# One Mish activation for the second layer's gate, and fp32r fillers of several widths in the opening, in an attention and two-layer MLP kernel

## The chip, the cores and the metric

The kernel runs on one core of a Trainium2 chip, as one program in one launch. The metric is the device time in microseconds. Before the change three runs gave 1089.35, 1090.94 and 1094.02 us, a median of 1090.94.

## The reference

```python
for t in range(S):                      # q, k, v, alpha: 4 x 8 x 768 x 48
    state = alpha[:, :, t, :, None] * state + np.einsum('bhd,bhe->bhde', k[:, :, t], v[:, :, t])
    y[:, :, t] = np.einsum('bhd,bhde->bhe', q[:, :, t], state)
x = y as 3072 tokens x 384
# first layer: 384 -> 2048 -> 384, weights float64
h = x @ w_in
g = (a[0] + a[1] * h + a[2] * h * h + a[3] * h**3) / (1 + abs(b[0]) * abs(h) + abs(b[1]) * h * h + 1e-6)
x = g @ w_out
# second layer: 384 -> 2048 -> 384, weights float64
h = x @ w_in
sp = np.where(h > 20.0, h, np.log1p(np.exp(np.minimum(h, 20.0))))
out = (h * np.tanh(sp)) @ w_out
```

The gate of the second layer, h * tanh(softplus(h)), is the function called Mish.

## The kernel before

The 3072 tokens are worked in six blocks of 512 (128 positions of four batches). Each layer goes over the six blocks, and in a block over 16 tiles of 128 hidden units: 96 steps a layer, 192 in all. A step has nine matmuls of 128x512 into a PSUM bank for the hidden tile (`hidden_mms`, L525: three slices of the 384 inputs, and for each the product of two float32 numbers that are split into a high and a low part, high by high, low by high and high by low), then the gate (`hidden`), the split of its result into a high part `gh` and a low part `gl` (`split_g`), and nine more matmuls into three output banks (`out_mms`, L585). After the 16 steps of a block the three output banks are copied out (`evacuate`, L596 and L598). Five banks (0 to 4) take hidden tiles once the attention is over, three (5 to 7) the outputs. The split tiles have a ring of five buffers by then, the tiles before the split a ring of eleven.

The first layer's steps run beside the attention of the next block, whose small matmuls (L352, L363, L434, L447, L482, L498) wait in turn for ScalarE and VectorE. The attention of the first block fills the opening, before the first step.

The gate of the first layer is a rational function on ScalarE, VectorE and GpSimd (L539 to L557). The gate of the second layer is computed as h * cos(2 arctan(sigmoid(-h))): sigmoid (L561) and arctan (L563) on ScalarE, a copy of h out of PSUM on VectorE (L562), then for three tiles at a time three sines (L568) between two loads of ScalarE's activation table, then the product by `tt` (L173 on VectorE, L175 on GpSimd, by the letters in `E_W`).

Weights come as float64 words and are made into split float32 by `load_w`: a transfer into one of two staging tiles `raw`, three integer operations on VectorE (L260, L262, L264), an Abs of the high words on ScalarE (L266), a product with its comparison on VectorE (L267), the cast to the high part on ScalarE (L180) and the difference to the low part on VectorE (L173: `wil` for the input weights, `wol` for the output weights). The sixteen loads of the second layer alternate: the first staging tile serves the input weights, the second the output weights. They overwrite the first layer's weights as these fall free, so they stand in the last block of the first layer and the first block of the second.

The order of everything is made beforehand. `Plan` takes each operation with its engine, an estimated length, a due time and what it reads and writes; `order()` plays the graph by these estimates, each engine taking, of what is ready, what is due first. The instructions are issued in that order, and each engine runs its own in that order. The due time of a step's output matmuls is its own plus `LAG` (40.27 us in the second layer), that of its split plus `D_SPL`. Table loads have an estimate only in `sines` (2.6 us for the two).

In the opening 120 matmuls that nothing needs (L635, "fillers") stand in the plan with the latest due times, so that TensorE takes one whenever nothing else is ready. The output matmuls of the first step use the same banks and come behind all of them. An fp32 matmul leaves two records in the trace.

Of the kernel before, what the change touches and what calls it, by code (L numbers as in the profile page):

```python
# [14 lines left out]
ALU = mybir.AluOpType  # L15
# [6 lines left out]
NP = H // 2            # head pairs  # L22
HC = 64                # state chunk
NBLK = S // P          # blocks of 4 x 128 tokens
NTOK = B * P           # tokens of a block
# [7 lines left out]
NLVM = 5               # levels that need a mask  # L33
T0, T_AT, T_MOE = (63.77, 5.28, 3.51)   # microseconds: the first step, a step with attention, one without
# [4 lines left out]
LAG, GRP = ((16.02, 40.27), (1, 3))  # L39
D_SIN, D_SPL = (16.46, (-2.71, 23.06))  # L40
NZX, NGX = (7, 2)
E_W = 'VVVPPV'
# [3 lines left out]
E_GL = ('PVPVVP', 'PVPPVV')  # L46
# [6 lines left out]
N_WARM = 120  # L53
D_CST = 5.0
NZ, NG, NU = 4, 3, 3   # buffers of the hidden tiles
C1 = 1.0 + 1e-6
# high word of the smallest float64 that is a normal float32, read as a float32
# [3 lines left out]
class Plan:  # L61
    """Instructions as a graph, ordered before they are issued.

    Operations are added in an order that is right; what they read and write gives the graph.
    order() plays them on the engines, by estimated times, each engine taking of its ready
    operations the one that is due first.
    """
# [3 lines left out]
    TICK, WARM = 3.413, 3060       # the clock of the tensor engine: columns in a tick that make the next one fast  # L71
# [76 lines left out]
def attention_moe_kernel(ctx: ExitStack, tc: tile.TileContext,  # L148
# [21 lines left out]
    def tt(eng, n, due, reads, writes, kw):  # L170
        """a product, sum or difference of two tensors on the vector engine or on GpSimd"""
        if eng == "V":
            dve(n, due, reads, writes, lambda: nc.vector.tensor_tensor(**kw()))  # L173
        else:
            pool(n, due, reads, writes, lambda: nc.gpsimd.tensor_tensor(**kw()))  # L175

    def copy(eng, n, due, reads, writes, out, in_):
        """a copy in SBUF"""
# [16 lines left out]
    c_2 = cpool.tile([P, 1], F32, name="c_2")  # L195
# [9 lines left out]

    us = [cpool.tile([P, NTOK], F32, name=f"u{j}") for j in range(NU)]

    def rings(pool, nz, ng, x):
        """buffers of the hidden tiles: before the split, and split"""
# [558 lines left out]
```

## Time and profile before

| | |
|---|---|
| median of three runs | 1090.94 us |
| profiled execution, first to last instruction | 1090.5 us |
| TensorE, ScalarE, VectorE, GpSimd busy | 94%, 86%, 75%, 30% |
| mean granted clock of TensorE | 0.992 |

The profiled execution has no time of its own beside its span of 1090.5 us, which lies 0.4 us under the median of the runs. A time in a row is counted from the span's start. PE is TensorE's matmuls, PEld its weight loads, DVE VectorE, ACT ScalarE, POOL GpSimd, SP SyncE, whose queue issues the transfers. A row of a group gives the line, the operation, what it writes and reads, the count, then busy time, the mean length of one, and the idle time of the engine ahead of them with what ended it. A matmul's length includes its way through the array and overlaps the next one's, so the pitch from start to start says what one costs. In a timeline the brackets give the idle time before an instruction.

### The profile page before, as it was taken

How to read it: one execution, taken by the hardware profiler on the slowest of the kernel's cores; microseconds unless marked ns; L12 is line 12 of the kernel's file. 1: busy time of each engine (PE TensorE's matmuls, PEld its weight loads, DVE VectorE, ACT ScalarE, POOL GpSimd, SP SyncE). 2: the span in 40 equal slices, each digit the busy share in tenths (PEclk: the TensorE clock that was granted, in tenths of full speed). 3: DMA queues.
4: the chain of work that ended last, by engine and by line, in shares of the span. 5: the costliest groups of instructions: out<-in, count | busy, mean ns of one | idle time of the engine just before them, and what ended most of it. 6: DMA issues, size and time to landing. Idle time of an engine off the chain costs nothing.

```text
span 1090.5 us, 24632 instructions
## 1 busy us (share of the span) xinstructions
PE 1030.2 (94%) x9912; PEld 806.5 (74%) x9912; DVE 814.8 (75%) x1266; ACT 933.7 (86%) x1788; POOL 323.1 (30%) x320
## 2 busy tenths in 40 slices
PE   6999887999899999999899999999999999999998
PEld 5767665777676777766677777778888888888886
DVE  7899999798898887877999699999884411234452
ACT  5789998999999998978788799899997988889773
POOL 4014454402012224332423134234101256643000
PEclk9999999899999999999999999999999999999999
DMA  6644142403050312113131111222110100000000
GB/s 206 204 138 145 45 155 73 147 15 109 17 185 17 98 54 90 58 56 105 57 99 36 60 58 49 88 97 98 48 58 1 59 1 29 30 19 10 1 29 29
DMA packets 28209, 78.31 MB, mean 72 GB/s; under 512 B 4160, under 2 KB 7360, under 8 KB 28096
## 3 DMA queue, kind: packets, MB, share of 16 engines
q1 hardware_dynamic: 28096, 76.75, 21.5%
q8 instruction: 78, 1.28, 0.5%
q14 instruction: 35, 0.29, 0.1%
HBM read 66.24 MB, written 9.44 MB: 69 GB/s over the span
## 4 chain that ended last, share of the span: by engine, by line
PE 39%; DVE 8%; ACT 5%; issue 1%; DMA 1%; POOL 0%; SPq 0%; DVEq 0%
PE bank L585 20%; PE bank L525 17%; DVE zx L542 1%; DVE p L548 1%; DVE px L557 1%; DMA raw<-in_w2i_dram 1%; DMA qka<-in_qT_dram 1%; ACT u L539 1%; DVE f L262 0%; DVE px L548 0%; DVE px L550 0%; DVE p L557 0%; PE bank L352 0%; DVE f L267 0%; DVE f L264 0%
## 5 line engine op out<-in xcount | busy, mean ns | idle before, releaser
L525 PE MATMUL bank<-xh,wih 128*128 128x512 f32 x576 | 234.8, 408 | 7.0 <-DVE px L550 3.0
L525 PE MATMUL bank<-xh,wil 128*128 128x512 f32 x576 | 225.6, 392 | 1.6 <-DVE wil L173 1.6
L525 PE MATMUL bank<-xl,wih 128*128 128x512 f32 x576 | 225.6, 392 | 0.0
L585 PE MATMUL bank<-gh,woh 128*128 128x512 f32 x444 | 184.1, 415 | 0.2 <-ACT u L598 0.2
L585 PE MATMUL bank<-gl,woh 128*128 128x512 f32 x444 | 175.6, 395 | 2.2 <-DVE gl L173 1.8
L585 PE MATMUL bank<-gh,wol 128*128 128x512 f32 x444 | 175.3, 395 | 0.4 <-DVE wol L173 0.4
L525 PEld LDWEIGHTS bank<-xh,wih 128*128 128x128 f32 x576 | 108.2, 188 | 32.5 <-DVE px L550 3.9
L525 PEld LDWEIGHTS bank<-xh,wil 128*128 128x128 f32 x576 | 108.4, 188 | 25.4 <-DVE wil L173 2.0
L525 PEld LDWEIGHTS bank<-xl,wih 128*128 128x128 f32 x576 | 108.6, 189 | 20.0 <-DVE xl L517 0.5
L175 POOL TENSOR_TENSOR gl<-p,gh 128x512 fp32r<-128x512 f32 x47 | 71.7, 1528 | 161.4 <-ACT gh L180 127.5
L334 ACT COPY Q<-qka 64x256 f32<-64x256 f32 x232 | 95.3, 411 | 26.9 <-DVE qka L319 14.5
L562 DVE COPY px<-bank 128x512 f32<-128x512 f32 x60 | 40.9, 688 | 85.7 <-PE bank L525 83.0
L546 POOL TENSOR_TENSOR z<-z,u 128x512 f32<-128x512 f32 x48 | 69.2, 1442 | 115.1 <-ACT z L545 114.5
L585 PEld LDWEIGHTS bank<-gh,wol 128*128 128x128 f32 x444 | 84.5, 190 | 19.5 <-DVE wol L173 0.8
L585 PEld LDWEIGHTS bank<-gh,woh 128*128 128x128 f32 x444 | 84.1, 189 | 19.4 <-ACT u L598 0.7
L585 PEld LDWEIGHTS bank<-gl,woh 128*128 128x128 f32 x444 | 84.6, 191 | 18.1 <-DVE gl L173 2.1
L352 PEld LDWEIGHTS bank<-Q,qka 128*31 128x31 f32 (+4 forms) x3840 | 39.5, 105 | 63.4 <-ACT Q L334 32.5
L548 DVE SCALAR_TENSOR_TENSOR p<-p,sc,bank 128x512 f32<-128x512 f32 x85 | 62.8, 740 | 17.9 <-ACT p L547 16.8
L352 PE MATMUL bank<-Q,qka 128*31 128x32 f32 (+4 forms) x3840 | 51.8, 197 | 24.4 <-ACT Q L334 10.0
L381 DVE TENSOR_TENSOR qka<-qka,qk 128x512 f32<-128x512 f32 x96 | 72.6, 764 | 1.6 <-PE bank L352 0.6
L539 ACT ACTIVATE u<-bank 128x512 f32<-128x512 f32 x96 | 57.2, 596 | 14.3 <-PE bank L525 12.6
L635 PE MATMUL bank<-cst 128*128 128x256 f32 x240 | 62.8, 400 | 6.0 <-DMA cst<-in_consts_dram 6.0
(117 smaller groups left out, 2235.9 us busy)
## 6 DMA issues: line engine op xcount, KB each, us to landing
qka<-in_kaT_dram SPq DMA_DIRECT2D x24, 512.0 KB, 5.2
qk<-in_nat_dram SPq DMA_DIRECT2D x24, 384.0 KB, 3.7
raw<-in_w1i_dram SPq DMA_DIRECT2D x8, 768.0 KB, 5.0
raw<-in_w1o_dram SPq DMA_DIRECT2D x8, 768.0 KB, 4.4
raw<-in_w2i_dram SPq DMA_DIRECT2D x8, 768.0 KB, 4.4
raw<-in_w2o_dram SPq DMA_DIRECT2D x8, 768.0 KB, 4.3
Q<-in_qT_dram SPq DMA_DIRECT2D x48, 96.0 KB, 2.4
qka<-in_qT_dram SPq DMA_DIRECT2D x48, 96.0 KB, 4.3
```

The source lines that it names most:

```text
L175: pool(n, due, reads, writes, lambda: nc.gpsimd.tensor_tensor(**kw()))
L334: act(2 * P, now(), [kQC], [kQ], lambda a=a, h=h: nc.scalar.copy(out=Qr[h, a], in_=Cr[h]), src="s")
L352: nc.tensor.matmul(lv[o:o + 32 - L, g, :, 16 * z:16 * z + 16].rearrange("p a (n l) -> p a n l", l=L), lhsT=K[:, g * P + o:g * P + o + 32 - L],
L381: dve(4 * P, now(), [kT[L]], [kQC, kK], lambda: nc.vector.tensor_tensor(out=QK, in0=QK, in1=Tv.rearrange("p m x -> p x m").unsqueeze(3).to ...
L525: nc.tensor.matmul(bank[hb], lhsT=w[f // 2][:, f % 2, k * P:(k + 1) * P], rhs=x[k], start=(k == 0 and j == 0), stop=(k == KT - 1 and j == 2))
L539: act(NTOK, due, [kh], [ku], lambda: nc.scalar.activation(u, h, AF.Abs))
L542: dve(NTOK, due, [ku], [kz], lambda: nc.vector.scalar_tensor_tensor(out=zs[r], in0=zs[r], scalar=B0, in1=u, op0=ALU.add, op1=ALU.mult), ptr=1)
L546: pool(NTOK, due, [ku], [kz], lambda: nc.gpsimd.tensor_tensor(out=zs[r], in0=zs[r], in1=u, op=ALU.mult))
L548: dve(NTOK, due, [kh], [kp], lambda: nc.vector.scalar_tensor_tensor(out=ps[r], in0=ps[r], scalar=A2, in1=h, op0=ALU.add, op1=ALU.mult), po ...
L562: dve(NTOK, due, [kh], [kp], lambda: nc.vector.tensor_copy(out=ps[r], in_=h), port=False)
L585: nc.tensor.matmul(bank[5 + k], lhsT=w[f // 2][:, f % 2, k * P:(k + 1) * P], rhs=x[q], start=(f == 0 and j == 0), stop=(f == FT - 1 and j ...
L635: nc.tensor.matmul(bank[5 + n % 3][:, 0:2 * P], lhsT=ident, rhs=cst[:, 0:2 * P], start=True, stop=True)
```

## The change

The second layer's gate becomes one activation that reads the hidden bank and writes the tile that is split. The sigmoid, the arctan, the sines with their table loads, the copy and the product go, and with them the grouping by three. The output matmuls of a second-layer step are due 10.2 us after the step and not 40.27, its split 0.9 us after and not 23.06. The differences `gl` of blocks 2 and 3 move from GpSimd to VectorE. The fillers read a tile of ones in place of the identity and the constants; each is a pair of fp32r matmuls, ten of one shape after ten of another, four shapes in turn, with an estimate of 0.45 us in place of 0.43. Comments are taken out, so that lines move up by up to 17.

```diff
-LAG, GRP = ((16.02, 40.27), (1, 3))
-D_SIN, D_SPL = (16.46, (-2.71, 23.06))
+LAG = (16.02, 10.2)
+D_SPL = (-2.71, 0.9)
 NZX, NGX = (7, 2)
-E_W = 'VVVPPV'
...
-E_GL = ('PVPVVP', 'PVPPVV')
+E_GL = ('PVPVVP', 'PVVVVV')
...
+WARM_FORM = ((128, 512), (128, 256), (128, 384), (96, 512))
...
-    c_2 = cpool.tile([P, 1], F32, name="c_2")
...
+    wtile = cpool.tile([P, NTOK], F32R, name="wtile")
...
         else:
-            # tanh(softplus(h)) = cos(2 arctan(sigmoid(-h)))
-            act(NTOK, due, [kh, "tables"], [kz], lambda: nc.scalar.activation(zs[r], h, AF.Sigmoid, scale=-1.0))
-            dve(NTOK, due, [kh], [kp], lambda: nc.vector.tensor_copy(out=ps[r], in_=h), port=False)
-            act(NTOK, due, [], [kz], lambda: nc.scalar.activation(zs[r], zs[r], AF.Arctan), src="s")
-
-    def sines(rs, due):
-        def emit():
-            for r in rs:
-                nc.scalar.activation(zs[r], zs[r], AF.Sin, scale=-2.0, bias=c_2)
-            nc.scalar.preload_act_table_set("sigmoid_and_others")
-
-        plan.add("ACT", 0.62 * len(rs) + 2.6, due, [], [f"z{r}" for r in rs], emit)
+            act(NTOK, due, [kh, "tables"], [kp], lambda: nc.scalar.activation(ps[r], h, AF.Mish))
 
     def split_g(l, r, q, i, due):
         c = steps[i][1]
-        kz, kp, kgh, kgl = f"z{r}", f"p{r}", f"gh{q}", f"gl{q}"
-        if l == 1:
-            tt(E_W[c], NTOK, due, [kz], [kp], lambda: dict(out=ps[r], in0=ps[r], in1=zs[r], op=ALU.mult))
+        kp, kgh, kgl = f"p{r}", f"gh{q}", f"gl{q}"
         copy(E_GH[l][c], NTOK, due, [kp], [kgh], lambda: ghs[q], lambda: ps[r])
         tt(E_GL[l][c], NTOK, due, [kp, kgh], [kgl],
            lambda: dict(out=gls[q], in0=ps[r], in1=ghs[q].bitcast(F32), op=ALU.subtract))
...
-        nc.vector.memset(c_2, 0.5 * math.pi)
...
+        nc.gpsimd.memset(wtile.bitcast(F32), 1.0)
...
     for n in range(N_WARM):
         def warm(n=n):
-            nc.tensor.matmul(bank[5 + n % 3][:, 0:2 * P], lhsT=ident, rhs=cst[:, 0:2 * P], start=True, stop=True)
-        pe(0.43, 1e6 + n, ["cst"], [f"bank{5 + n % 3}"], warm)
+            w, x = WARM_FORM[n // 10 % len(WARM_FORM)]
+            tw, tx = wtile[:, 0:w], wtile[:, 0:x]
+            for j in range(2):
+                nc.tensor.matmul(bank[5 + n % 3][0:w, 0:x], lhsT=tw, rhs=tx, start=True, stop=True)
+        pe(0.45, 1e6 + n, ["cst"], [f"bank{5 + n % 3}"], warm)
...
-    pend = []
     for i, (l, c, f) in enumerate(steps):
         if f == 0:
             if l == 1:
@@ -673,19 +661,14 @@
         hidden_mms(hb, f, V[i])
         nz, ng = (NZ, NG) if i < FT * (NBLK - 1) else (NZ + NZX, NG + NGX)
         hidden(l, hb, i % nz, i, V[i] + D_MID)
-        pend.append((l, c, f, i, i % nz, i % ng))
-        if len(pend) == GRP[l] or i + 1 in (L1N, len(steps)):
-            if l == 1:
-                sines([x[4] for x in pend], V[i] + D_SIN)
-            for l, c, f, i, r, q in pend:
-                split_g(l, r, q, i, V[i] + D_MID + D_SPL[l])
-                out_mms(f, q, V[i] + LAG[l])
-                if f == FT - 1:
-                    evacuate(l, c, V[i] + LAG[l] + D_EV)
-                if l == 0 and c == NBLK - 1 and f % 2 == 1:
-                    load_w(w2i, wi_h, wi_l, "wi", f // 2, V[i] + D_IN)
-                    load_w(w2o, wo_h, wo_l, "wo", f // 2, V[i] + D_OUT)
-            pend.clear()
+        r, q = i % nz, i % ng
+        split_g(l, r, q, i, V[i] + D_MID + D_SPL[l])
+        out_mms(f, q, V[i] + LAG[l])
+        if f == FT - 1:
+            evacuate(l, c, V[i] + LAG[l] + D_EV)
+        if l == 0 and c == NBLK - 1 and f % 2 == 1:
+            load_w(w2i, wi_h, wi_l, "wi", f // 2, V[i] + D_IN)
+            load_w(w2o, wo_h, wo_l, "wo", f // 2, V[i] + D_OUT)
```

The planner's result is a new order. The first place is on TensorE, at the first output step of the second layer (`bank5` from `woh0`); `wih`, `wil` are the high and low input weights, two steps to a number. Before:

```order
L525 MATMUL bank2_121<-xh2_109,wih5_75 128x512
L525 MATMUL bank2_121<-xl2_112,wih5_75 128x512
L525 MATMUL bank2_121<-xh2_109,wil5_83 128x512
L585 MATMUL bank5_124<-gh1_139,woh0_86 128x512
L585 MATMUL bank5_124<-gl1_142,woh0_86 128x512
L585 MATMUL bank5_124<-gh1_139,wol0_94 128x512
```

And now:

```order
L524 MATMUL bank3_121<-xh2_108,wih3_72 128x512
L524 MATMUL bank3_121<-xl2_111,wih3_72 128x512
L524 MATMUL bank3_121<-xh2_108,wil3_80 128x512
L571 MATMUL bank5_123<-gh1_139,woh0_85 128x512
L571 MATMUL bank5_123<-gl1_142,woh0_85 128x512
L571 MATMUL bank5_123<-gh1_139,wol0_93 128x512
```

The first output step stood behind twelve hidden steps (up to input weights 5) and now stands behind eight (up to 3).

The second place is on ScalarE, where the last block of the first layer is copied out of banks 5 and 7 (`u0`, `u2`), the second layer's first gates are made and weights are converted. Before:

```order
L563 ACTIVATE z1_131<-z1_131 128x512
L598 COPY u0_127<-bank5_124 128x512
L568 ACT_TABLE_LOAD
L568 ACTIVATE zx4_7428<-zx4_7428,c_2_68 128x512
L568 ACTIVATE zx5_7429<-zx5_7429,c_2_68 128x512
L568 ACTIVATE zx6_7430<-zx6_7430,c_2_68 128x512
L569 ACT_TABLE_LOAD
L266 ACTIVATE raw0_102<-raw0_102 128x768
L598 COPY u2_129<-bank7_126 128x512
L266 ACTIVATE raw1_103<-raw1_103 128x768
L561 ACTIVATE z2_132<-bank1_120 128x512
L180 CAST wih6_76<-f320_104 128x768
```

And now:

```order
L559 ACTIVATE p2_136<-bank1_119 128x512
L265 ACT_TABLE_LOAD
L265 ACTIVATE raw1_102<-raw1_102 128x768
L265 ACTIVATE raw0_101<-raw0_101 128x768
L559 ACT_TABLE_LOAD
L559 ACTIVATE p3_137<-bank2_120 128x512
L179 CAST wih6_75<-f320_103 128x768
L584 COPY u0_127<-bank5_123 128x512
L179 CAST woh1_86<-f321_104 128x768
L584 COPY u2_129<-bank7_125 128x512
L179 CAST gh0_138<-p1_135 128x512
```

The sines with their two table loads are gone; a load now stands ahead of the Abs of `raw` and another ahead of the next Mish (L559). There are 17 such loads in all.

The third place is on VectorE, behind the sixth low input weight (`wil5`). Before:

```order
L173 TENSOR_TENSOR wil5_83<-f320_104,wih5_75 128x768
L562 COPY px5_7436<-bank2_121 128x512
L562 COPY px6_7437<-bank3_122 128x512
L562 COPY p0_134<-bank4_123 128x512
L562 COPY p1_135<-bank0_119 128x512
L260 TENSOR_SCALAR f320_104<-raw0_102 128x768
L173 TENSOR_TENSOR wol0_94<-f321_105,woh0_86 128x768
L262 SCALAR_TENSOR_TENSOR f320_104<-raw0_102,f320_104 128x768
L260 TENSOR_SCALAR f321_105<-raw1_103 128x768
L264 SCALAR_TENSOR_TENSOR f320_104<-raw0_102,f320_104 128x768
L596 COPY u1_128<-bank6_125 128x512
L262 SCALAR_TENSOR_TENSOR f321_105<-raw1_103,f321_105 128x768
```

And now:

```order
L172 TENSOR_TENSOR wil5_82<-f320_103,wih5_74 128x768
L172 TENSOR_TENSOR wol0_93<-f321_104,woh0_85 128x768
L259 TENSOR_SCALAR f321_104<-raw1_102 128x768
L259 TENSOR_SCALAR f320_103<-raw0_101 128x768
L261 SCALAR_TENSOR_TENSOR f321_104<-raw1_102,f321_104 128x768
L261 SCALAR_TENSOR_TENSOR f320_103<-raw0_101,f320_103 128x768
L263 SCALAR_TENSOR_TENSOR f321_104<-raw1_102,f321_104 128x768
L263 SCALAR_TENSOR_TENSOR f320_103<-raw0_101,f320_103 128x768
L266 SCALAR_TENSOR_TENSOR f320_103<-raw0_101,f320_103 128x768
L266 SCALAR_TENSOR_TENSOR f321_104<-raw1_102,f321_104 128x768
L582 COPY u1_128<-bank6_124 128x512
L172 TENSOR_TENSOR wil6_83<-f320_103,wih6_75 128x768
```

The copies of hidden tiles (L562) are gone, and the conversions of `raw0` and `raw1` stand directly behind one another.

## Rows read from the trace of the kernel before

**Rows 1.** The page: busy time and share of each engine; the chain by line.

```profile
PE 1030.2 (94%) x9912; PEld 806.5 (74%) x9912; DVE 814.8 (75%) x1266; ACT 933.7 (86%) x1788; POOL 323.1 (30%) x320
...
PE bank L585 20%; PE bank L525 17%; DVE zx L542 1%; DVE p L548 1%; DVE px L557 1%; DMA raw<-in_w2i_dram 1%; DMA qka<-in_qT_dram 1%; ACT u L539 1%; DVE f L262 0%; DVE px L548 0%; DVE px L550 0%; DVE p L557 0%; PE bank L352 0%; DVE f L267 0%; DVE f L264 0%
```

**Rows 2.** By stretches: length, busy us (x) of each engine, clock, DMA share, GB/s.

```profile
100.00:600.00 500.00, 463.87 (x6313) 346.97 (x6312) 438.49 (x724) 451.85 (x981) 159.46 (x178) 0.98 0.25 77
...
640.00:680.00 40.00, 36.70 (x158) 29.04 (x157) 39.96 (x52) 37.32 (x65) 15.58 (x8) 1.00 0.13 41
...
800.00:840.00 40.00, 40.00 (x178) 33.13 (x177) 23.93 (x41) 32.31 (x45) 2.54 (x2) 1.00 0.07 20
...
695.00:780.00 85.00, 82.76 (x362) 67.30 (x361) 78.59 (x98) 82.41 (x125) 27.76 (x18) 1.00 0.27 93
```

**Rows 3.** The chain in order of time, near its end: start, us, what.

```profile
1062.16 24.49 PE bank L585 x108
```

**Rows 4.** TensorE: a group's row for 640 to 740 us, then its timeline (start, us).

```profile
L525 PE MATMUL bank<-xh,wih 128*128 128x512 f32 x74 | 29.1, 394 | 4.1 <-DVE px L550 3.0 <-DVE p L550 1.1
...
698.06 0.50 PE L585 MATMUL bank<-glx,woh 128*128 128x512 f32 x1 [0.65 <-POOL glx L175]
...
726.79 0.39 PE L525 MATMUL bank<-xl,wih 128*128 128x512 f32 x1
728.77 0.50 PE L525 MATMUL bank<-xh,wil 128*128 128x512 f32 x1 [1.59 <-DVE wil L173]
729.11 0.39 PE L525 MATMUL bank<-xh,wih 128*128 128x512 f32 x1
...
983.66 0.50 PE L585 MATMUL bank<-gh,woh 128*128 128x512 f32 x1 [0.23 <-ACT u L598]
```

**Rows 5.** ScalarE and VectorE by groups, 695 to 780 us: xcount, busy us, mean ns.

```profile
L563 ACT ACTIVATE zx<-zx 128x512 f32<-128x512 f32 x17 | 10.5, 630 | 0.0
L561 ACT ACTIVATE zx<-bank 128x512 f32<-128x512 f32 x17 | 9.8, 592 | 0.1
L568 ACT ACT_TABLE_LOAD x7 | 9.0, 1283 | 0.1
L568 ACT ACTIVATE zx<-zx,c 128x512 f32<-128x512 f32 x13 | 8.5, 714 | 0.0
L266 ACT ACTIVATE raw<-raw 128x768 f32<-128x768 f32 x8 | 7.2, 907 | 0.1
L568 ACT ACTIVATE z<-z,c 128x512 f32<-128x512 f32 x8 | 5.3, 715 | 0.0
L563 ACT ACTIVATE z<-z 128x512 f32<-128x512 f32 x8 | 4.9, 632 | 0.0
...
L562 DVE COPY px<-bank 128x512 f32<-128x512 f32 x16 | 10.6, 682 | 1.3 <-PE bank L525 1.3
```

**Rows 6.** SyncE's queue: issues of the second layer's output weights: start, us.

```profile
727.27 10.75 SPq L259 DMA_DIRECT2D raw<-in_w2o_dram  x2
...
737.70 0.33 SPq L259 DMA_DIRECT2D raw<-in_w2o_dram  x1
...
750.39 0.33 SPq L259 DMA_DIRECT2D raw<-in_w2o_dram  x1
```

**Rows 7.** ScalarE's timeline at a table load: start, us, instruction.

```profile
978.46 1.28 ACT L568 ACT_TABLE_LOAD   x1
979.76 0.72 ACT L568 ACTIVATE z<-z,c 128x512 f32<-128x512 f32 x1
```

**Rows 8.** The opening: TensorE's timeline, and one stretch of all engines.

```profile
14.54 0.46 PE L352 MATMUL bank<-Q,qka 128*31 128x32 f32 x32 [1.10 <-POOL qk L175]
...
50.49 3.62 PE L635 MATMUL bank<-cst 128*128 128x256 f32 x16
...
91.92 0.59 PE L525 MATMUL bank<-xh,wih 128*128 128x512 f32 x1
...
24.00:36.00 12.00, 10.95 (x213) 8.19 (x212) 11.75 (x20) 9.32 (x25) 0.00 (x0) 1.00 0.21 71
```

More of the change, by code (lines that the diff above doesn't have):

```diff
@@ L1 @@
-import math
 import heapq
```

## The prediction

> **What bounds the kernel now.** I read the page's shares first. TensorE is busy 94% of the span, ScalarE 86%, VectorE 75%, and the chain that ended last is mostly two lines of TensorE, the matmuls into the hidden tiles (L525) and out of them (L585) [rows 1]. A share is an average over stages, so the table by stretches comes next [rows 2]: from 100 to 600 us (first layer beside the attention) TensorE is busy 464 of 500 us; from 640 to 680 it has 36.7 of 40 while VectorE has 39.96; from 800 to 840 it has 40.00 of 40. So there are three stages: one mixed, one short stage where VectorE (weights of the second layer still to convert, polynomials of the first still to finish) holds up TensorE, and a long one in which TensorE alone is the limit.
>
> How full is "full"? The chain ends with 108 output matmuls in 24.49 us, 0.2268 us each with nothing between [rows 3]. One step of the second layer is 18 of them, 4.08 us; 96 steps are 392 us. The change removes none of these matmuls. What it can give back in the second layer is only what TensorE waits there, and the timeline shows that [rows 4]. Each idle time costs itself plus 0.27: before 728.77 the idle time is 1.59, but start to start it is 1.98 in place of 0.23 (1.75 lost), and the next matmul comes 0.34 later in place of 0.23. Three waits between 668 and 685 us are for the first layer's polynomials (VectorE, L550): 3.0 + 1.1 us idle in the groups' row, 4.9 with the 0.27 each. Those at 698.06 (0.65 for GpSimd's difference), 728.77 (1.59 for a low weight half) and 983.66 (0.23 for an evacuation that stood behind a table load on ScalarE) are in the part that the change rewrites: 0.92 + 1.86 + 0.50 = 3.3 us. Smaller ones are left out.
>
> **The change part by part.**
>
> *The activation.* Per hidden tile it removes on ScalarE an arctan (0.63) and a sine, and two table loads of 1.283 per three tiles; on VectorE a copy from PSUM (0.68) and a product [rows 5]. It adds nothing per tile but turns the sigmoid (0.59) into a Mish. No row has a Mish; as it is one pass from the same bank, I bound it by the sigmoid's 0.59 and the arctan's 0.63 and take 0.59. After 780 us all this is off the path: TensorE is the limit there, and neither engine's relief shortens a matmul. It is worth 0.50 us there (983.66). The end isn't shortened either: the last hidden matmul of before is followed by 108 output matmuls, that of after by 27, but the 81 others only move ahead of it. The three steps that remain, 6.1 us, still cover the last tile's activation, cast and difference (0.6 + 0.6 + 0.7 and three handovers).
>
> *Table loads that the plan doesn't know.* ScalarE's new order has a load around each of the eight Abs that the weights of the second layer still need: 17 loads in all, of which 16 are these pairs. In before the same eight Abs of 0.907 need none, and 14 sine-group loads stand in the same 85 us [rows 5]. So the sum on ScalarE there falls: it loses 14 x 1.283 + 25 arctans (15.4) + 21 sines (13.8) = 47 us and gets 17 x 1.283 = 22. ScalarE was busy 82.4 of 85 us in this stretch, VectorE 78.6 [rows 2]; both get room. But the plan puts the loads nowhere, so each pair delays what stands behind it by 2.57 us. Two places matter. (a) The evacuation of the first layer's last block (banks 5 and 7) stands behind one such pair, and TensorE now comes to the first output step after 8 hidden steps, not 12. I charge half a pair, 1.2 us; the bounds are 0 and 2.6. (b) The conversion of an output weight waits for its Abs, now behind a load. In before one such conversion, from transfer to transfer, takes 10.4 us (727.27 to 737.70) to 12.7 (737.70 to 750.39) [rows 6], with VectorE and ScalarE full. After, the queueing shrinks and 1.28 comes in: I take 10.4, between 9.1 (10.4 less the load, if the queue was worth two) and 14.0 (12.7 and the load). TensorE uses one such weight per 36 to 51 matmuls in the new order, 8.2 to 11.6 us, on average 10.2. That is even; I charge 0.8 us for the one place with 36, and 0 to 12 as bounds.
>
> The Trainium skill (ScalarE: Activation LUTs, section "Table sets: the hidden batching unit") says that cheap functions, abs among them, are in every set. By that there would be one load and no (a) or (b), and the sum would be 2 us lower. The instructions as built have the pairs, so I go by them.
>
> *A load's price.* The row shows a load of 1.28 us at 978.46, and the sine behind it starts at 979.76, 0.02 us after its end [rows 7]. The same page of the Trainium skill (section "What ACT_TABLE_LOAD costs") puts a switch at about 2.66 us, a drain included. By the row a pair is 2.57 us, by the page 5.3, which would push (b) to 11.8 us and into the second rival below. The row decides.
>
> *Order and buffers.* Up to VectorE's sixth low weight half of the second layer (wil5, at 696 us) the order of before and after is the same there, so I keep the 4.9 us of waits ahead of it. Behind it VectorE goes straight into weights: wil7 is 19 rows after wil5, in before 39. That is why I count the 1.59 at 728.77 as gone. The 0.65 at 698.06 goes too: six more hidden matmuls stand before that output step. With the lag of output steps cut from about ten steps to three, output weights are wanted 4 hidden steps earlier: that is (b) above.
>
> *The fillers.* 120 fillers of one fp32 128x256 matmul (two records) become 120 pairs of fp32r matmuls. Before: 16 records in 3.62 us, (3.62 - 0.38) / 15 = 0.216 each, so 0.432 a filler, 51.8 us in all [rows 8]. After: a 512-wide pair is 0.45 by the pitch above (60 fillers). No row has a narrower fp32r matmul; by columns a 256-wide pair is 0.23 and a 384-wide 0.34, and if width changed nothing both are 0.45. So 44 to 54 us; by columns 44. TensorE's time is not what ends the opening: VectorE is busy 11.75 of 12 us at 24 to 36 [rows 8]. A shorter filler helps only where an attention group is ready and has to wait until a filler ends: 22 groups in a row on one stream (two units of 11), each held 0.22 us on average (half a filler), 4.7 us; the mean filler falls by a fifth at most, so 0.9 us gained. Bounds: 4.7 gained, 2.6 lost (54.4 - 51.8). They now wait for GpSimd's memset of their operand and not for the constants' transfer; the first attention group comes at 14.54 either way, as it waits for a product on GpSimd.
>
> The planned length of a filler also goes from 0.43 to 0.45, which shuffles the order of the first layer locally. I have no row that gives this a sign; 0, with 4 us to either side.
>
> *Sum.* 1090.5 (span of the profiled execution) - 3.3 + 1.2 + 0.8 - 0.9 = 1088.3. The median of the runs is 0.4 us above that span and the runs differ by 4.7 us, so I say 1088.
>
> **Rivals.**
>
> 1. *The room is worth more.* The order gets ahead on the output weights, (a) and (b) cost nothing, and the opening gives its whole 4.7: 1090.5 - 3.3 - 4.7 = 1082.5; with 1 to 2 us from the shuffle, 1081. For it: both full engines lose a third of their work in 695 to 780. Against: VectorE, not TensorE, ends the opening.
>
> 2. *The output weights take over as the wait (slower).* Each conversion's Abs waits for a load, and the next load keeps a Mish and a cast from running, so a conversion stays at 12.7 us, as in the widest row. It decides from 10.2 us on, the mean time in which TensorE uses one up: five weights x 2.5 = 12.5 us in place of my 0.8: 1100. For it: only one of the two staging buffers serves the output weights, so nothing overlaps. Against: the queues that made 12.7 out of 10.4 are the ones that are relieved.
>
> 3. *The narrow fillers leave TensorE idle and its clock falls.* In 100 to 600 us the granted clock is 0.98 [rows 2]: about 10 us lost to stretches at 1.2 GHz, in the stage where TensorE has gaps; the opening's was 1.00 with fillers that filled every planned slot. After, a 256-wide pair fills 0.23 of 0.45 us. Twelve us at half clock, wholly exposed, are 6 us: 1094; with a bad shuffle 1097. Against: at the lower clock the fillers are twice as long and fill the slots again, and VectorE ends the opening anyway.
>
> 4. *It changes nothing*: the waits gone are made up by (a) and (b), 1091. It is within my forecast's range.
>
> **How the numbers follow.** Forecast with the fourth 0.58 (its own range 1085 to 1093), first rival 0.20, second 0.13, third 0.09. Half a per cent, 5.5 us, is about what a measurement of this kernel tells from no change; so faster means under 1085.5, slower over 1096.4. Faster: the first rival and 0.06 of the forecast, 0.26. Slower: the second, and 0.04 of the third, 0.17. Same: 0.57. Range 1081 to 1098: it leaves out the far half of the first and of the second.
>
> **What would show it.** Right: after about 780 us TensorE without idle time at 0.2268 a matmul; the three L550 waits of 1.1 to 1.5 still there; no wait for wil7; sixteen loads of 1.28 around the Abs; a wait of 1 to 2 us of the first output step for the evacuation. The opening: the first hidden matmul near 91 us (91.92 in before, [rows 8]). Wrong: output steps that wait for low output weights over 1 us several times (second rival), a granted clock under 1.00 before 90 us (third), the first hidden matmul at 88 or earlier (first), or a first layer that is 4 us longer or shorter.

## The result: slower, and the profile after

The changed kernel takes 1104.95 us (median of 4 runs, 1102.51 to 1105.87) against 1092.2 us for the kernel before in the same series: 1.012 of it, with a 95% interval of 1.0097 to 1.0142. The forecast was 1088, with a range up to 1098. The profiled execution spans 1103.8 us against 1090.5, so 13.3 us have to be found where the forecast had 2.2 gained.

In the page of after, the first part answers to [rows 1]: busy time, share of the span and instructions of each engine.

```profile
PE 1034.4 (94%) x9912; PEld 807.0 (73%) x9912; DVE 742.9 (67%) x1137; ACT 766.2 (69%) x1548; POOL 244.7 (22%) x257
```

ScalarE has lost 168 us of work and VectorE 72, and the time went up. The shares tell nothing of why; TensorE's stays at 94%. The table by stretches answers to [rows 2].

```profile
100.00:600.00 500.00, 461.30 (x6225) 342.28 (x6224) 441.20 (x715) 449.38 (x974) 163.87 (x180) 0.98 0.24 77
640.00:680.00 40.00, 38.21 (x166) 30.66 (x165) 39.93 (x53) 38.30 (x67) 15.38 (x9) 1.00 0.18 59
...
800.00:840.00 40.00, 40.00 (x178) 33.14 (x177) 16.22 (x29) 5.37 (x9) 0.00 (x0) 1.00 0.11 40
```

From 100 to 600 us TensorE issued 88 matmuls fewer than before in the same 500 us, two of them a filler's: the first layer, in which the source changes nothing but the fillers, fell behind. From 640 to 680 VectorE is still full (39.93 of 40). From 800 to 840 TensorE is full as before, with ScalarE nearly idle (5.37 of 40) and VectorE at 16.22. The chain of waits after (start, us, what, number) ends so, where [rows 3] had 108 output matmuls at 0.2268:

```profile
1071.40 2.04 PE bank L524 x9
1093.84 6.13 PE bank L571 x27
```

That is 0.227 a matmul as well. What splits the 13.3 us best is the start of TensorE's first hidden matmul of some blocks, read from its timeline in every kernel of this study (us). "Layer 2" is that of the second layer's first step, the last column the time from there to the start of the last output matmul.

| kernel | first block | second block | layer 2 | layer 2 to the end |
|---|---|---|---|---|
| before | 91.9 | 210.4 | 675.0 | 411.2 |
| after | 94.0 | 221.6 | 683.3 | 416.3 |
| 1 fillers, planned at 0.45 | 94.4 | 220.3 | 681.3 | 410.9 |
| 2 planned at 0.45 alone | 94.3 | 222.0 | 683.5 | 410.9 |
| 3 fillers, planned at 0.43 | 91.9 | 210.4 | 674.5 | 410.9 |
| 4 Mish alone | 93.1 | 208.7 | 671.9 | 415.2 |
| 5 after with Square | 94.6 | 220.1 | 682.0 | 413.0 |
| 6 Mish and Square | 91.9 | 208.7 | 672.6 | 413.1 |
| 7 Mish, evacuation first | 91.7 | 208.8 | 670.8 | 416.0 |
| 8 Mish, Square, evacuation first | 92.5 | 209.6 | 671.2 | 410.3 |
| 9 order of 0.43, then 0.45 | 92.2 | 220.5 | 681.1 | 411.3 |
| 10 order of 0.45, then 0.43 | 93.1 | 213.8 | 678.6 | 410.8 |
| 11 planned at 0.41 | 93.4 | 218.5 | 680.6 | 410.9 |
| 12 after, both places mended | 91.1 | 210.5 | 673.4 | 410.0 |

So 8.2 us are lost before the second layer starts, all of it by the second block (11.2 there, of which 3.0 come back), and 5.1 after, where 1.3 were to be gained. Each row is one execution. Kernels with the same first-layer order (before, 3, 4, 6, 7, 8 and 12) start the second layer up to 4 us apart, 670.8 to 675.0, so the first part is known only that well. The last column is steadier: the seven kernels with the old gate lie between 410.8 and 411.3.

**The seam between the layers.** TensorE's waits of after from 665 to 780 us (who waits for whom: us, times, longest) answer to [rows 4]:

```profile
PE bank L571 <- ACT u L584: 3.8, 1, 3.8
PE bank L524 <- DVE px L549: 3.0, 2, 1.5
PE bank L524 <- DVE p L549: 1.1, 1, 1.1
PE bank L571 <- DVE wol L172: 0.5, 2, 0.3
PE bank L571 <- ACT woh L179: 0.2, 1, 0.2
```

The waits for VectorE's polynomials (3.0 + 1.1) are there again. Those for wil and for GpSimd's difference are gone. The output weights show 0.7 us of idle time, but cost more from start to start, as TensorE's timeline of after shows at the first of them:

```profile
760.67 0.39 PE L524 MATMUL bank<-xh,wil 128*128 128x512 f32 x1
761.30 0.50 PE L571 MATMUL bank<-ghx,woh 128*128 128x512 f32 x1 [0.24 <-ACT woh L179]
761.64 0.40 PE L571 MATMUL bank<-glx,woh 128*128 128x512 f32 x1
762.29 0.50 PE L571 MATMUL bank<-ghx,wol 128*128 128x512 f32 x1 [0.26 <-DVE wol L172]
```

The starts are 0.63, 0.34 and 0.65 apart in place of 0.23. There are five such places up to 786 us (two of them too short for the list), 2.2 us in all. New is the first row of the list: the second layer's first output step waits for the evacuation of the first layer's last block (L584). ScalarE's timeline of after (start, us, instruction, idle time before and its releaser) shows what the copy stood behind:

```profile
710.17 1.28 ACT L265 ACT_TABLE_LOAD   x1
712.23 0.91 ACT L265 ACTIVATE raw<-raw 128x768 f32<-128x768 f32 x1 [0.77 <-DVE f L261]
714.20 0.90 ACT L265 ACTIVATE raw<-raw 128x768 f32<-128x768 f32 x1 [1.06 <-DVE f L261]
715.11 1.28 ACT L559 ACT_TABLE_LOAD   x1
716.40 0.60 ACT L559 ACTIVATE p<-bank 128x512 f32<-128x512 f32 x1
718.11 0.83 ACT L179 CAST wih<-f 128x768 fp32r<-128x768 f32 x1 [1.10 <-DVE f L266]
718.85 0.58 ACT L584 COPY u<-bank 128x512 f32<-128x512 f32 x1
```

There are two suspects: the two loads of 1.28 (as long as in [rows 7], successor 0.01 us behind), and the three waits for VectorE, 2.93 us together. On TensorE the same place costs more than the wait:

```profile
715.24 0.39 PE L524 MATMUL bank<-xh,wil 128*128 128x512 f32 x1
719.48 0.79 PE L571 MATMUL bank<-gh,woh 128*128 128x512 f32 x1 [3.85 <-ACT u L584]
720.07 0.63 PE L571 MATMUL bank<-gl,woh 128*128 128x512 f32 x1
...
724.76 0.45 PE L524 MATMUL bank<-xh,wih 128*128 128x512 f32 x1
725.05 0.39 PE L524 MATMUL bank<-xl,wih 128*128 128x512 f32 x1
```

After an idle time of 3.85 us the matmuls come 0.43 us apart until 724.76, then 0.23 again: the granted clock was at the lower of its two levels (1.2 GHz) from 718.0 to 724.8. The wait takes 4.0 us, the clock about 2.8 more.

### The profile page after: what moved, and what is told of

Its sections match the earlier page's. It is cut to its first block, busy times and chain, and to the rows that moved or that the text cites. A ratio compares the mean times of both kernels' runs of the same rounds, so it can differ in the third digit from the quotient of the medians.

```text
span 1103.8 us, 24160 instructions
## 1 busy us (share of the span) xinstructions
PE 1034.4 (94%) x9912; PEld 807.0 (73%) x9912; DVE 742.9 (67%) x1137; ACT 766.2 (69%) x1548; POOL 244.7 (22%) x257
## 3 DMA queue, kind: packets, MB, share of 16 engines
q8 instruction: 78, 1.28, 0.5%
## 4 chain that ended last, share of the span: by engine, by line
PE 46%; ACT 26%; DVE 19%; issue 4%; DMA 3%; POOL 1%; SPq 0%; DVEq 0%; ACTq 0%; POOLq 0%
PE bank L571 22%; PE bank L524 18%; ACT Q L333 4%; DVE qka L380 2%; ACT z L551 2%; ACT u L538 2%; ACT p L546 2%; ACT gh L179 2%; DVE AT L405 2%; DVE p L556 2%; DMA qka<-in_qT_dram 2%; DVE p L547 2%; ACT z L555 2%; ACT AT L396 2%; PE bank L351 1%
## 5 line engine op out<-in xcount | busy, mean ns | idle before, releaser
L559 ACT ACTIVATE px<-bank 128x512 f32<-128x512 f32 x60 | 35.7, 598 | 136.5 <-PE bank L524 136.5
L174 POOL TENSOR_TENSOR gl<-p,gh 128x512 fp32r<-128x512 f32 x40 | 62.3, 1558 | 165.0 <-ACT gh L179 129.6
L172 DVE TENSOR_TENSOR gl<-p,gh 128x512 fp32r<-128x512 f32 x65 | 48.3, 743 | 54.0 <-ACT gh L179 53.7
L172 DVE TENSOR_TENSOR gl<-px,gh 128x512 fp32r<-128x512 f32 x31 | 21.4, 692 | 76.9 <-ACT gh L179 76.7
```

Source lines behind the costliest of these rows:

```text
L559: act(NTOK, due, [kh, "tables"], [kp], lambda: nc.scalar.activation(ps[r], h, AF.Mish))
```

## The experiments

All were timed beside the kernel before on the same chip; ratios are to it, with 95% intervals. Runs 1 to 4 shared one series (before: 1092.85 us), 5 to 8 another (1090.06), 9 to 12 a third (1091.24).

### 1 to 4: the parts apart

Fillers with the new planned length; the planned length alone; the fillers with the old one; the gate alone (fillers as before). The edit that tells 1 and 3 apart, and that alone makes 2 out of the kernel before:

```diff
-        pe(0.43, 1e6 + n, ["cst"], [f"bank{5 + n % 3}"], warm)
+        pe(0.45, 1e6 + n, ["cst"], [f"bank{5 + n % 3}"], warm)
```

> The kernel before with the new fillers alone (fp32r pairs of four shapes, estimate 0.45); the second layer's gate is the old one. Up to the second layer's first hidden step the changed kernel is 8.3 us late. If the fillers with their estimate cause that, this runs at about 1100 us, with the first hidden matmul near 94 us and the clock at half in the opening. If what is lost there were lost by the gate's change, it runs at 1091.

Measured: 1099.43 us, 1.0063 (1.0037 to 1.0089).

> The kernel before with one number changed: a filler is planned at 0.45 us in place of 0.43; the fillers are the old fp32 ones. Instruction order on TensorE, ScalarE and VectorE is then that of the run with the new fillers alone. Theory 'order': the 8 us come from the shuffled first layer, and this runs at 1098 to 1100. Theory 'clock': narrow fillers let the clock fall, and this runs at 1091 to 1092 with a granted clock of 1.00 in the opening.

Measured: 1097.96 us, 1.0056 (1.003 to 1.0081). Not one instruction differs from the kernel before, only their order.

> The kernel before with the new fillers but planned at 0.43 us, so that the order on TensorE, ScalarE and VectorE is word for word that of before. Theory 'clock': falls to half between 14 and 70 us as in the changed kernel, 1094 to 1099. Theory 'order': within 1 us of before, 1090 to 1092.

Measured: 1091.22 us, 0.9996 (0.9977 to 1.0015). So the new fillers cost and gain nothing that shows within 0.2%. Yet they let the clock fall, as this kernel's table of the opening shows (length, busy us of TensorE, its weight loads, VectorE, ScalarE and GpSimd, then the clock):

```profile
0.00:20.00 20.00, 12.25 (x138) 10.19 (x139) 12.63 (x22) 9.71 (x26) 11.55 (x28) 0.89 0.87 279
20.00:60.00 40.00, 34.52 (x607) 26.54 (x606) 34.66 (x54) 29.42 (x74) 5.27 (x8) 0.93 0.56 176
60.00:90.00 30.00, 28.80 (x488) 21.67 (x489) 27.61 (x45) 25.34 (x69) 1.97 (x8) 0.94 0.47 158
24.00:36.00 12.00, 10.62 (x211) 6.99 (x209) 11.69 (x20) 9.66 (x25) 0.00 (x0) 1.00 0.24 77
```

The clock is 0.89 to 0.94 of full where before had 1.00, and the first hidden matmul starts at 91.90 us, against 91.92 [rows 8]. The last row points to the reason: from 24 to 36 us VectorE is as full as before (11.69 of 12, before 11.75), so TensorE is not the limit there. Over 20 to 60 us neither is full (34.66 and 34.52 of 40).

> The changed kernel with the old fillers (fp32, 0.43): the gate's change alone. From the second layer's first hidden step to the end the changed kernel loses 5.0 us against before. If the gate's change does that by itself, this runs at 1095 to 1096 us, with an idle time near 4 us of TensorE ahead of the first output step of the second layer and a clock at half behind it. If that stall hung on the fillers' shuffle, it runs at 1088, as forecast without the fillers.

Measured: 1093.85 us, 1.0021 (1.0000 to 1.0042). That is below the 1095 to 1096 expected. In the profiled execution the gate's kernel is 3.1 us ahead at the second layer's start, which is spread (the order up to there is that of before), and takes 4.0 us more than before behind it, with the same wait for the evacuation (3.8 us). That is 1.1 less than in after; the half-clock stretch behind the wait is 3.4 us here (at 707.7) and 6.8 there.

The clock of the opening is thereby ruled out as the cause of a loss of this size, and two causes stand: the order, about 6 us, and the seam, which takes more than the gate gives.

### 5 to 8: what the evacuation waits for

The square of a weight's high word, compared with the square of the bound, marks the same weights as its magnitude; with it the compiled kernel has 2 table loads in place of 18 (one of the 18 is at the start, one ahead of the first Mish, sixteen stand around the Abs).

```diff
-        act(n, due, [], [kr], lambda: nc.scalar.activation(mag, mag, AF.Abs), src="s")
+        act(n, due, [], [kr], lambda: nc.scalar.activation(mag, mag, AF.Square), src="s")
...
-            out=st, in0=mag, scalar=F64_MIN, in1=st, op0=ALU.is_ge, op1=ALU.mult))
+            out=st, in0=mag, scalar=F64_MIN ** 2, in1=st, op0=ALU.is_ge, op1=ALU.mult))
```

> The changed kernel (1104.95 us), with Square in place of Abs in the step that marks the smallest weights (and the square of the bound it is compared with), so that ScalarE needs no other function table between two Mish: 2 table loads in place of 18, all orders as in the changed kernel. Theory A, the last block's evacuation is late by the table loads before and behind Abs: the wait of the first output matmul of the second layer (4.01 us at 715) falls by the 2.56 us of two loads to some 1.4, the half-clock stretch of 6.8 us behind it goes or halves (3 us), span 1103.8 to some 1098 to 1101, time 1099 to 1102. Rival B, it is late because it stands in ScalarE's queue behind two Abs and a conversion that wait for VectorE (0.77, 1.06 and 1.10 us of idle time there): the loads only fill time in which ScalarE would wait anyway, the wait stays above 3 us, time 1103 to 1105. Either way the 8 us that are lost by block 1 stay.

Measured: 1104.16 us, 1.0137 (1.0110 to 1.0164); the wait for the evacuation is 3.9 us, as with all the loads. The profiled execution was the fastest of the four (1101.20 us).

> The Mish gate alone (old fillers, old order, 1093.85 us) with Square in place of Abs: 2 table loads in place of 18. Theory A (loads): the evacuation's wait of 3.8 us at the seam falls to some 1.3, the half-clock stretch at 707.7 goes (1.7 us), time 1089 to 1091, under the kernel before (1092.9). Rival B (place in the queue): wait above 3 us, time 1092.5 to 1094.

Measured: 1091.98 us, 1.0022 (1.0006 to 1.0038), against 1.0021 with the loads. The wait is the same 3.8 us, and ScalarE's timeline of this kernel shows where the loads' time went:

```profile
701.60 0.90 ACT L263 ACTIVATE raw<-raw 128x768 f32<-128x768 f32 x1 [2.07 <-DVE f L259]
703.57 0.91 ACT L263 ACTIVATE raw<-raw 128x768 f32<-128x768 f32 x1 [1.07 <-DVE f L259]
704.38 0.58 ACT L557 ACTIVATE p<-bank 128x512 f32<-128x512 f32 x1
707.49 0.83 ACT L178 CAST wih<-f 128x768 fp32r<-128x768 f32 x1 [2.52 <-DVE f L264]
708.23 0.58 ACT L582 COPY u<-bank 128x512 f32<-128x512 f32 x1
```

Waits of 0.76, 1.07 and 1.09 us in run 4 have become 2.07, 1.07 and 2.52: 2.74 us more, about the 2.56 that two loads took. The loads had filled time in which ScalarE waits for VectorE anyway. Theory A is refuted for this wait.

The loads weren't free everywhere, though. The last column of the table falls with Square from 415.2 to 413.1 (4 and 6) and from 416.3 to 413.0 (after and 5). In both pairs the five places where TensorE waited for output weights, 2.2 us, are gone; the other 1.1 of the second pair goes with a half-clock stretch of 3.4 us in place of 6.8. Two microseconds are 0.2%, which the ratios of 4 and 6 cannot tell.

Next, the copies' place in the queue, without and with Square. The copies go right behind the last output matmul that they read, and the last of the weights' steps on ScalarE ahead of them, with all that follows from it, goes behind them (`first` holds the copies, `mags` those steps):

```diff
+        for n in self.first:                # as soon as what it reads is issued
+            out.remove(n)
+            out.insert(max(out.index(d) for d in ops[n][3]) + 1, n)
+        p = max(out.index(n) for n in self.first)
+        behind = {max((n for n in self.mags if out.index(n) < p), key=out.index)}     # the last of the weights' steps on ScalarE ahead of them
+        for n in out[:p]:
+            if ops[n][3] & behind:
+                behind.add(n)
+        out = [n for n in out[:p + 1] if n not in behind] + [n for n in out[:p + 1] if n in behind] + out[p + 1:]
```

> The Mish gate alone (1093.85 us) with Abs and all its table loads kept, one pair more than there (20 loads in place of 18), but with the three evacuation copies of the first layer's last block moved ahead of the last Abs and the conversions that follow from it. Theory B (place in the queue): the first copy ends some 3 us earlier, the wait of 3.8 us falls to some 0.7, the half-clock stretch goes, time 1089 to 1091. Rival A (what counts is how many loads there are): no gain, 1093 to 1095. A third way, C: the weights that are now converted later become the wait (hidden matmuls for wih, wil), 1092 to 1094, with that wait in the list.

Measured: 1094.96 us, 1.0053 (1.0034 to 1.0072): slower than without the edit. The list of TensorE's waits (660 to 790 us) shows the third way of the expectation, though for an output weight and not for wih or wil:

```profile
PE bank L579 <- ACT woh L187: 2.9, 2, 2.7
PE bank L579 <- DVE u L590: 1.1, 1, 1.1
```

The evacuation's wait fell from 3.8 to 1.1, now for the copy on VectorE, and an output weight that is converted later became a wait of 2.7.

> The Mish gate alone with both edits, Square in place of Abs and the evacuation ahead of the last of the weights' steps. If loads and place in the queue add (A and B both), the wait of the first output matmul is below 0.4 us and the time 1087 to 1090, the three waits ahead of the first Mish-free stretch (the hidden tiles' banks, 3 to 4.5 us with the clock) remaining. If one of them is all, it is the same as the better of the two runs before, within 0.7 us. If the weights' conversions become late (C), 1091 to 1094.

Measured: 1087.66 us, 0.9982 (0.9965 to 0.9998): the fastest kernel of the study. Its waits in the same stretch, and two lines of ScalarE's timeline:

```profile
PE bank L532 <- DVE px L557: 3.0, 2, 1.5
PE bank L579 <- DVE u L590: 1.3, 1, 1.3
PE bank L532 <- DVE p L557: 1.1, 1, 1.1
PE bank L579 <- DVE wol L180: 0.4, 1, 0.4
```

```profile
701.41 0.58 ACT L592 COPY u<-bank 128x512 f32<-128x512 f32 x1
702.23 0.59 ACT L592 COPY u<-bank 128x512 f32<-128x512 f32 x1 [0.24 <-PE bank L579]
```

The second copy now waits for TensorE and not the other way round. The expected 0.4 us was too low: VectorE's copy of the middle bank still stands behind weights. With the copies in front, the loads do count (7 against 8): 7.3 us in the medians. The two profiled executions differ by 5.7 us from the second layer's start on (416.0 and 410.3), and TensorE's starts account for them: 2.9 for the weight's wait of 2.7, 1.8 for the stretch at half clock behind it, at 728.2, and 2.2 for the five later waits for output weights, less 1.2 that run 8 waits for output weights itself. The other 1.6 of the medians is not located. The edit on the queue was worth its time only where the loads were gone.

### 9 to 11: where the order loses

Runs 9 and 10 join the planner's two orders of the kernel before at one step. `a` is the order up to the step and `b` the one from it, `mark` is the step, and `s` is what stands ahead of it in the order of 0.43:

```diff
+        a, b = (self.play(us) for us in WARM_US)
+        n = KEEP.index(True)
+        cut = (a, b)[n].index(self.mark)
+        s = set((a, b)[n][:cut])
+        out = [x for x in a if x in s] + [x for x in b if x not in s]
```

> The kernel before, all its operations as they are; the order that the planner makes with the filler estimate 0.43 up to the ninth step of the first layer's first block, and from there the order that it makes with 0.45. The order of 0.45 as a whole costs 1.0056 (some 6 us). Theory D (the loss is made where the last units of block 0 meet block 1's attention on TensorE's queue): block 1 starts some 8 to 11 us later than the 210.4 us of before, and the time is 1.004 to 1.008 of before. Rival E (it is made in the opening, whose order moved by 0.02 us a filler, and only shows later): 0.998 to 1.002. Rival F (it is spread over all blocks): 1.003 to 1.006 without a step in the first block.

Measured: 1099.1 us, 1.0070 (1.0048 to 1.0092).

> The same turned around: the order of 0.45 up to what stands ahead of block 1's first step in the order of 0.43, and the order of 0.43 from there. Theory D: block 1 starts 5 to 11 us late, 1.003 to 1.007 of before, since the loss is made by then; but less than the whole if it is the place of block 1's scan ahead of block 0's last transposes that makes it, for these stand as before here. Rival E: 1.004 to 1.007. Rival F: 1.000 to 1.002.

Measured: 1095.95 us, 1.0038 (1.0017 to 1.0058).

The second block starts 10.0 us late in 9 and 3.4 late in 10; with the whole order of 0.45 it was 11.6, each known to some 2 us (with the order of 0.43 the block starts between 208.7 and 210.5). So most of it comes from the end of the first block and its meeting with the second: by run 9 all but 1.6 us, by run 10 all but 3.4. Run 9 refutes rival E, that the opening alone makes the loss; run 10 shows that what stands ahead of the meeting costs something too. In time the two do not add up to the whole: 9 alone costs what the order of 0.45 does (1.0070 and 1.0056), and 10 still 1.0038. The place is seen on TensorE's timeline, first of before:

```profile
202.37 1.14 PE L498 MATMUL bank<-vn,AT 64*64 64x48 f32 x32
...
205.61 0.81 PE L434 MATMUL bank<-cst,vn 128*128 128x128 f32 x6
...
210.43 0.39 PE L525 MATMUL bank<-xh,wih 128*128 128x512 f32 x1
```

Then of run 2, the order of 0.45 and nothing else:

```profile
205.87 1.13 PE L498 MATMUL bank<-vn,AT 64*64 64x48 f32 x32
207.16 0.55 PE L434 MATMUL bank<-cst,vn 128*128 128x128 f32 x3
...
213.51 0.46 PE L352 MATMUL bank<-Q,qka 128*31 128x32 f32 x32 [2.47 <-ACT Q L334]
...
215.40 0.49 PE L434 MATMUL bank<-cst,vn 128*128 128x128 f32 x3
...
218.71 0.66 PE L352 MATMUL bank<-Q,qka 128*31 128x32 f32 x32 [2.12 <-ACT xf L508]
...
222.02 0.41 PE L525 MATMUL bank<-xh,wih 128*128 128x512 f32 x1
```

L498 are the last attention outputs of the first block, L434 the transposes that its result still needs (3 for each of two units), L352 the first products of the *second* block's attention. In before both units are transposed 3.2 us after the last outputs began. In run 2 a product of the next block stands between them; the second unit is transposed 9.5 us after, and the hidden step that needs its tokens starts 11.6 us later than before. What that product waits for, on the DMA queue, VectorE and ScalarE of run 2:

```profile
203.34 2.44 SPq L303 DMA_DIRECT2D qka<-in_qT_dram  x1
...
206.30 0.47 SPq L304 DMA_DIRECT2D qka<-in_qT_dram  x1
...
211.81 0.43 DVE L319 TENSOR_TENSOR qka<-qka 128x256 f32<-128x256 f32 x1 [0.47 <-DMA vn<-in_nat_dram]
...
213.03 0.42 ACT L334 COPY Q<-qka 64x256 f32<-64x256 f32 x1
```

The product needs two such transfers. The first issue takes 2.44 us where its like takes 0.4, and what held it is not shown; the second goes out at 206.30 and lands at 211.62, and VectorE's first step on both starts at 211.81, 5.5 us after that issue. (The view puts the end of VectorE's idle time down to a transfer of vn, but that one lands at 212.42 by the same trace.) The planner counts 2.0 us and the bytes' time for a transfer, 2.3 for this one; the median of these issues from 200 to 214 us is 5.2 to landing. By the planner's clock the product was ready in time; on the chip everything behind it on TensorE waits, the current block's last transposes included. In run 9 the same group of products waits 4.70 us at 213.47, the longest wait there; in run 10 it stands behind the second block's first step, the second unit is transposed at 211.37, and no wait between 197 and 214 us is over 0.5. The two runs and the timelines point to this product's place as what costs most; no run moves it alone.

> The kernel before with the filler's estimate at 0.41 us in place of 0.43, as far below as the change went above; the fillers themselves as before. If the order of 0.43 is one of many draws of which it is the best that was looked for (theory G), this one is slower as well, 1.002 to 1.008 of before, by waits at other places in the first layer. If 0.45 was a bad draw among like ones (rival H), 0.997 to 1.002.

Measured: 1097.57 us, 1.0062 (1.0039 to 1.0084): as much as 0.45 costs, at other places. TensorE's waits from 94 to 225 us are, in front:

```profile
PE bank L525 <- DVE p L557: 8.0, 5, 4.0
PE bank L585 <- DVE wol L173: 3.5, 2, 3.1
```

### 12: the whole change with both places mended

The changed kernel with 0.43 for the planner, Square, and the evacuation's copies in front.

> The changed kernel with all its parts (Mish gate, fp32r fillers of several widths), with the planner told 0.43 us a filler, Square in place of Abs, and the last block's evacuation ahead of the last of the weights' steps on ScalarE. If order and seam are all that the change cost, it takes what the Mish gate alone with the two edits took, 1086 to 1090, some 0.996 to 1.000 of before; block 1 starts near 210 and the last output matmul near 1081.5. If the fillers cost by themselves once the order is mended (a clock near 0.9 until 60 us), 1090 to 1094.

Measured: 1089.44 us, 0.9985 (0.9965 to 1.0005). The second block starts at 210.5, the last output matmul at 1083.4, 1.9 us later than expected. Run 8 is the same kernel with the old fillers, and the intervals lie on each other. With order and seam mended nothing is left of the 1.2%. The gain behind them, about 2 us by both medians, is at the edge of the noise: the interval of 12 takes in 1.

The parts alone add up to less than the whole. Runs 1 and 4 cost 0.63% and 0.21%, 0.84% together, and the change 1.20% (0.97 to 1.42). The other 0.36%, some 4 us, is within what the three intervals leave open, and no run tests whether order and seam make each other worse.

## Why the prediction was wrong

Two steps failed, and only together do they take the time out of the range. The first adds 6 us to the 1088, which gives 1094; the second, with the output weights, adds some 7, which gives 1095; both give some 1101.

*The step that failed first is the shuffle of the first layer's order*, put at "0, with 4 us to either side". Run 2 gives it 5.1 us against the runs beside it, and 0.30% to 0.81% by its interval, 3.3 to 8.9 us. The forecast's own sign for it, a first layer that is 4 us longer, came (8.2 us in after). I had taken a planner's small change for noise around zero. But 0.43 isn't the middle of anything: 0.41 and 0.45 are both slower by about 0.6%, and the order of 0.43 was worth those 6 us. Three values don't make a distribution; they show that "no sign" was the wrong reading of a number that had no row.

*The second is the evacuation, term (a)*, 1.2 us between 0 and 2.6: it cost 4.0 us, with the clock's 2.8 on top. The place was right. The bounds were made from the one thing that the change adds in that queue, a pair of loads, and left out what the instructions there wait for, VectorE, which the rows had as full [rows 2]. As runs 6 to 8 show, the loads' own time was hidden there, and the queue's order was the price. The Trainium skill says in "PSUM — Partial Sum Buffer", section "Engine vs sequencer instructions", that the queues of ScalarE, VectorE and GpSimd are strictly first in, first out; the trace of after agrees, with a copy that starts at 718.85, behind a conversion, although the last matmul into its bank started at 712.52. And I priced a wait of TensorE at itself plus 0.27, from waits up to 1.6 us; this one, of 3.85, cost a stretch at 1.2 GHz as well.

*The output weights, term (b)*, 0.8 us: the five waits cost 2.2 us from start to start, and nothing with Square (runs 5 and 6), so it is the loads that make them, as the term has it, but for more than its one place. The rival that made them the bound did not come in the changed kernel, though run 7 shows that it was near, at 2.7 us for one weight.

*The waits that go*, 3.3 us: the 1.86 for wil and the 0.92 are gone, the polynomials' three stay, and behind 786 us there is no idle time and 0.227 a matmul. With the seam mended (12) the part from the second layer's start to the end is 1.2 us shorter than before. My sum of 3.3 less 1.2 and 0.8 was 1.3. There it is 3.7 gone (with two smaller waits of before, at 754.9 and 776.2 us), less 1.6 for the copy on VectorE and 1.0 for output weights, in a kernel without the sixteen loads that the sum was made for; the agreement is luck.

*The fillers*, -0.9 us: no gain at the first hidden matmul (91.90 against 91.92), and run 3's time cannot tell 0.9 from 0. That they would not decide the opening came out so (that VectorE ends it is shown for 24 to 36 us alone), and the third rival had the clock right and its price wrong: it falls, and costs nothing measurable. What I read as that rival's sign, a clock under 1.00 before 90 us, says nothing by itself.

Summed over the profiled execution of after: 8.2 up to the second layer; there -3.7 + 6.8 + 2.2 = 5.3, where 5.1 were measured.

## What to carry to other kernels

A number that only a planner reads is part of the kernel: before a change is judged, hold the old order and change the rest, then change the order alone. Price an instruction that is late in a queue by what the ones ahead of it wait for, not by what they take; work added ahead of such a wait may be free there, and taking it away may give nothing, while the same work costs where nothing else is waited for. A difference of 2 us that the time cannot tell may still be seen in a stage that repeats within 0.5 us. Behind a long idle time of TensorE, look at the granted clock before the next few microseconds are called full speed.

## What was not expected of the hardware

- Sixteen table loads of 1.283 us, 20.5 us of ScalarE's time at the seam, could not be seen in the time while the copies stood where they did (1.0021 with them, 1.0022 without); from the second layer's start on the traces show 2.1 us of them (415.2 and 413.1).
- A clock between 0.89 and 0.94 over the first 90 us, against 1.00, moved the first hidden matmul by 0.02 us (run 3 against before, one execution of each).
- A Mish on 128x512 from PSUM takes 0.598 us, as a sigmoid did (0.592).
- A filler's matmul of 384 columns took 0.173 us from start to start (ten from 91.80 to 93.53 us in after), near the 0.170 that its columns would give at 0.2268 for 512.
